# Second MoE's output products in a fused delta-rule, Mish-MoE and hard-swish-MoE kernel: weights stationary, 512 tokens moving

## Chip, cores and metric

One Trainium2 chip, one of its cores. The metric is the device time of the kernel in microseconds. All tensors are float32.

## What is computed

A delta-rule attention over 4 batches, 8 heads, 768 steps and head size 48 gives 3072 tokens of 384 features. Two feed-forward layers follow, each 384 -> 2048 -> 384:

```
h = k_n·state; state += beta * k_n ⊗ (v - h); y_t = q_t · state      (per batch and head, in order of t)
x  = y as (batch * seq, heads * head_dim)                            (3072, 384)
h1 = x @ w1_in;   x2  = (h1 * tanh(softplus(h1))) @ w1_out           first MoE (Mish)
h2 = x2 @ w2_in;  out = (h2 * clip(h2 + 3, 0, 6) / 6) @ w2_out       second MoE (hard-swish)
```

## The kernel before, in words

**Split numbers.** TensorE works on a float32 form of reduced precision (fp32r). Each operand is therefore kept as a high part and a low part, and each product of two float32 matrices is three products: high x high, high x low, low x high. In names, `xh`/`xl` are the parts of the tokens, `wih`/`wil` of the input weights, `ghi`/`glo` of the activated hidden values, `woh`/`wol` of the output weights.

**Blocks and units.** The 3072 tokens go through each MoE in 6 blocks of 512 (`n` is 0 to 5 in the first MoE, 6 to 11 in the second). The 2048 hidden features are 16 slices of 128 (`f`). One block and one slice make a unit, `u = 16 n + f`. A unit has two groups of products:

- hidden products, `mm1` (line 1285): weights are loaded into TensorE (stationary), the 512 tokens move through. 3 slices of the 384 input features x 3 splits = 9 products of 128x512, into one PSUM bank `hps`;
- output products. In the first MoE, `mm2_t` (line 1306): weights stationary, 512 hidden values move, 3 slices of 128 output features x 3 splits = 9 products of 128x512 into three banks `o0` to `o2`, which hold output features in partitions and tokens in columns. In the second MoE, `mm2_second` (line 1444): here the hidden values are stationary, 128 tokens at a time, and the 384 columns of the output weights move: 4 groups of tokens x 3 splits = 12 products of 128x384 into four banks `o0` to `o3` (in the trace `p`), which hold tokens in partitions.

The banks collect over the 16 units of a block. Between hidden and output products ACT and VectorE work on each unit. In the second MoE (`finish2`): ACT `r` (line 1417) and VectorE `r` (line 1419) read `hps` and form the hard-swish, ACT writes `ghi` (line 1291), VectorE writes `glo` (line 1425).

**Ends of blocks.** `flush1` (first MoE) copies the three banks to SBUF and stores them to a DRAM buffer `x2d`, features in partitions; `load_x2` (line 1410) loads a block of it for the second MoE as `x2in`, and `make_x` (lines 1263, 1267) splits it. `flush2` (second MoE, the first five blocks) copies the four banks, two with ACT (line 1459) and two with VectorE (line 1457), into `osb`, and stores them to `out` with four DMAs (line 1464), one for each batch. `last_out` does the same for the last block, cut in two halves. `osb` has three buffers in turn.

**Order.** Every engine executes its instructions in a fixed order. A small planner (`Flow`) writes it: each flow is a Python generator that yields an event to wait for or a tuple of engine and estimated duration, and the planner picks the flow that can begin earliest, corrected by hand-set penalties. `moe` issues the products of the units: the hidden group of unit `u`, then the output group of an earlier one. At a boundary the groups go: two output groups of the old block, the new block's first hidden group, the old block's last output group, two hidden groups in a row, the new block's first output group; elsewhere hidden and output groups alternate. `mm2_t` issues the low products of a unit last, except in the last unit of a block, where it goes bank by bank.

Of the kernel before, what the change touches and what calls it, by code (L numbers as in the profile page):

```python
# [8 lines left out]
F32 = mybir.dt.float32  # L9
# [3 lines left out]
ACTF = mybir.ActivationFunctionType  # L13
# [3 lines left out]
C = 32  # L17
# [126 lines left out]
def tile_delta_rule__moe_mish__moe_hardswish(  # L144
# [12 lines left out]
    nc = tc.nc  # L157
    B, H, S, D = q.shape
    NT, DM = out.shape
    DFF = w1_in.shape[1]  # L160
    KD = DM // 128
    KF = DFF // 128
# [5 lines left out]
    NB = NS // 4  # L168
# [14 lines left out]
    with tc.manual_schedule():  # L183
# [3 lines left out]
        ps_o = ctx.enter_context(tc.tile_pool(name="ps_o", bufs=1, space=bass.MemoryType.PSUM))  # L187
# [963 lines left out]
        wi, wo = {}, {}  # L1151
# [102 lines left out]
        xhl, acc = {}, {}  # L1254
# [36 lines left out]
            nc.scalar.activation(out=hi, in_=g, func=ACTF.Copy)  # L1291
            return hi, lo

        def mm2_t(i, f, hi, lo):
            g, e = divmod(f, 4)
            wh, wl = wo[1, g]
            ops = [(dc, x) for dc in range(KD) for x in range(3)]
            if f < KF - 1:
                ops.sort(key=lambda z: z[1] == 2)
            for n, (dc, x) in enumerate(ops):  # L1300
                if n % 3 == 0:
                    yield "PE", 3 * MM, 0
                if n == 0 and f == 0:
                    acc[i] = [ps_o.tile([128, 512], F32, tag=f"o{z}", name=f"o{z}") for z in range(KD)]
                w, a = ((wh, hi), (wl, hi), (wh, lo))[x]
                nc.tensor.matmul(out=acc[i][dc], lhsT=w[:, e, 128 * dc:128 * (dc + 1)], rhs=a,  # L1306
                                 start=(f == 0 and x == 0), stop=(f == KF - 1 and x == 2))
# [33 lines left out]
        def mm2_first(u):  # L1341
            i, f = divmod(u, KF)
            yield f"lo1.{7 * (f // 4) + KD + f % 4}"
            yield f"g{u}"
            if f == 0 and i:
                yield f"flush{i - 1}"
            if u == 0:
                for b in ("o0", "o1", "o2"):
                    yield lambda: bank_at[b]
            yield from mm2_t(i, f, *gs.pop(u))  # L1350
            flow.set(f"mm2.{u}")
            if f == KF - 1:
                flow.add(flush1(i), pen=-0.2)
# [8 lines left out]
        def moe():  # L1362
# [32 lines left out]
            while done < 2 * NB * KF - 1:  # L1395
                done += 1
                yield from mm2_second(done)
# [31 lines left out]
        def mm2_second(u):  # L1429
            n, f = divmod(u, KF)  # L1430
            g, e = divmod(f, 4)
            yield f"lo2.{7 * g + KD + e}"
            yield f"g{u}"
            if f == 0:
                yield f"flush{n - 1}"
            yield "PE", 12 * 0.1745, 0
            if f == 0:
                acc[n] = [(ps_o if s < 3 else ps_b).tile([128, DM], F32, tag=f"o{s}", name=f"p{s}") for s in range(4)]
            hi, lo = gs.pop(u)
            wh, wl = wo[2, g]  # L1440
            for s in range(4):
                c = slice(128 * s, 128 * (s + 1))
                for x, (a, w) in enumerate(((hi, wh), (hi, wl), (lo, wh))):
                    nc.tensor.matmul(out=acc[n][s], lhsT=a[:, c], rhs=w[:, e, :],  # L1444
                                     start=(f == 0 and x == 0), stop=(f == KF - 1 and x == 2))
            flow.set(f"mm2.{u}")
            if f == KF - 1:
                flow.add((flush2 if n < 2 * NB - 1 else last_out)(n), pen=-0.2)

        def flush2(n):  # L1450
            a, i = acc.pop(n), n - NB
            yield "lo2.27"
            o = p2.tile([128, 4, DM], F32, tag=f"r{i % 3}", name="osb")
            for s in range(4):
                yield ("DVE.", 0.55) if s % 2 else ("ACT", 0.5)
                if s % 2:
                    nc.vector.tensor_copy(out=o[:, s, :], in_=a[s])
                else:
                    nc.scalar.activation(out=o[:, s, :], in_=a[s], func=ACTF.Copy)
            flow.set(f"flush{n}")  # L1460
            yield "SP", 0.3
            for b in range(B):
                r0 = b * S + 128 * i
                nc.sync.dma_start(
                    out=out[r0:r0 + 128, :].rearrange("(t s) d -> s t d", s=C),
                    in_=o[C * b:C * (b + 1)],
                )

        def last_out(n):
            a, i = acc.pop(n), n - NB  # L1470
# [50 lines left out]
        p2 = ps_b = None  # L1521
# [21 lines left out]
        for m, lower, val in ((maskl, True, -1.0), (masku, False, 1.0)):  # L1543
# [4 lines left out]
            for b in range(B):  # L1548
                p = slice(C * b, C * (b + 1))
                nc.gpsimd.tensor_copy(out=m[p, :], in_=lt[p, p])  # L1550
        for b in range(B):
            p = slice(C * b, C * (b + 1))
# [143 lines left out]
```

## Time and profile before

| | |
|---|---|
| median of 3 runs | 1020.66 us (1019.56 to 1022.0) |
| the profiled execution's own time | 1023.31 us |
| its span, from the first to the last instruction | 1021.3 us |
| mean granted TensorE clock | 0.994 of full speed |
| TensorE products, busy | 990.8 us (97%) |
| VectorE / ACT / GpSimd, busy | 646.2 / 487.9 / 87.4 us |
| output products of the second MoE (line 1444) | 1152 of 128x384 |
| second MoE's first output product / last block's first | at 620.40 / 955.00 us |

The profile is of one execution. Products overlap in TensorE's pipeline, so that an instruction's own duration (some 0.34 or 0.39 us) is longer than the distance between two starts; what a product costs is read from starts. In the chain of waits, a piece's start lies at the end of the first product's issue and its length reaches to the next piece, so these pieces can be compared with each other. DVE is VectorE, SPq is the SyncE queue that issues DMAs, PEclk the granted TensorE clock (1.00 is 2.4 GHz).

### The profile page before, as it was taken

The page shows a single profiled execution, that of the slowest core. Times are in us where ns is not written, and L with a number is a line of the kernel's source. Part 1 is how long each engine was busy: PE and PEld are TensorE (multiplying, and loading weights), DVE is VectorE, ACT ScalarE, POOL GpSimd, SP SyncE. Part 2 cuts the span into 40 slices and gives each one's busy share as a digit, 9 for nine tenths or more (in the row PEclk, how much of TensorE's full clock was granted, in tenths as well). Part 3 has the DMA queues.
Part 4 walks back from the last instruction along what each step waited for, and adds up shares of the span by engine and source line. Part 5 has one row for each costly group of instructions (what it writes and reads, how often), then busy time and mean ns, then how long its engine had stood idle before and what let it go on. Part 6 is the DMA issues. An engine that isn't in the chain of part 4 may idle for free.

```text
span 1021.3 us, 29630 instructions
## 1 busy us (share of the span) xinstructions
PE 990.8 (97%) x12563; PEld 828.2 (81%) x12584; DVE 646.2 (63%) x1581; ACT 487.9 (48%) x1164; POOL 87.4 (9%) x132
## 2 busy tenths in 40 slices
PE   7888999999999999999999999999999999999997
PEld 5466777877887887788788888999999989999997
DVE  7999899875887688597527889543343333433432
ACT  4456588736655564564225566343343333433332
POOL 3242112102202110110000000000000000000000
PEclk9998999999999999999999999999999999999999
DMA  4644545245435654543133534011020020200101
GB/s 84 164 90 127 148 117 122 55 80 87 69 83 82 103 117 70 96 91 82 30 103 95 180 125 165 1 31 32 1 62 1 1 62 1 62 1 1 31 1 31
DMA packets 207156, 73.66 MB, mean 72 GB/s; under 512 B 189968, under 2 KB 193040, under 8 KB 207024
## 3 DMA queue, kind: packets, MB, share of 16 engines
q1 hardware_dynamic: 205696, 71.27, 30.7%
q8 instruction: 99, 1.62, 0.7%
q10 hardware_dynamic: 1328, 0.49, 0.2%
q14 instruction: 33, 0.27, 0.1%
HBM read 55.74 MB, written 15.99 MB: 70 GB/s over the span
## 4 chain that ended last, share of the span: by engine, by line
PE 82%; DVE 11%; ACT 3%; issue 2%; DMA 1%; POOL 0%; SPq 0%; DVEq 0%; ACTq 0%; POOLq 0%
PE hps L1285 36%; PE p L1444 20%; PE o L1306 16%; DVE sbd L943 2%; PE ksps L880 1%; PE gps L489 1%; PE dsps L932 1%; PE ups L890 1%; DVE tmp L847 1%; DVE late L708 1%; DVE tw L701 1%; PE yps L880 1%; PE yps L900 1%; DVE tp L851 1%; PE qps L777 1%
## 5 line engine op out<-in xcount | busy, mean ns | idle before, releaser
L1285 PE MATMUL hps<-xh,wih 128*128 128x512 f32 x576 | 229.7, 399 | 3.6 <-ACT mt L511 2.1
L1285 PE MATMUL hps<-xh,wil 128*128 128x512 f32 x576 | 227.0, 394 | 0.0
L1285 PE MATMUL hps<-xl,wih 128*128 128x512 f32 x576 | 226.6, 393 | 0.0
L1419 DVE SCALAR_TENSOR_TENSOR r<-r,hps 128x512 f32<-128x512 f32 x96 | 66.0, 688 | 173.6 <-ACT r L1417 173.5
L1417 ACT ACTIVATE r<-hps,half_c 128x512 f32<-128x512 f32 x96 | 66.1, 689 | 166.2 <-PE hps L1285 166.0
L1285 PEld LDWEIGHTS hps<-xh,wih 128*128 128x128 f32 x576 | 108.4, 188 | 27.2 <-ACT mt L511 2.7
L1444 PE MATMUL p<-woh,glo 128*128 128x384 f32 x384 | 129.5, 337 | 0.0
L1444 PE MATMUL p<-woh,ghi 128*128 128x384 f32 x384 | 129.2, 337 | 0.0
L1444 PE MATMUL p<-wol,ghi 128*128 128x384 f32 x384 | 128.9, 336 | 0.0
L1285 PEld LDWEIGHTS hps<-xh,wil 128*128 128x128 f32 x576 | 108.3, 188 | 23.7 <-DVE wil L1250 0.4
L1285 PEld LDWEIGHTS hps<-xl,wih 128*128 128x128 f32 x576 | 108.4, 188 | 19.3 <-DVE xl L1267 0.3
L1316 ACT ACTIVATE g<-hps 128x512 f32<-128x512 f32 x96 | 57.0, 594 | 127.2 <-PE hps L1285 126.8
L1306 PE MATMUL o<-ghi,wol 128*128 128x512 f32 x288 | 114.3, 397 | 0.0
L1306 PE MATMUL o<-ghi,woh 128*128 128x512 f32 x288 | 114.0, 396 | 0.0
L1325 DVE TENSOR_TENSOR glo<-g,ghi 128x512 fp32r<-128x512 f32 x96 | 66.5, 692 | 59.7 <-ACT ghi L1291 59.0
L1425 DVE TENSOR_TENSOR glo<-r,ghi 128x512 fp32r<-128x512 f32 x96 | 66.5, 693 | 58.9 <-ACT ghi L1291 58.1
L1291 ACT ACTIVATE ghi<-r 128x512 fp32r<-128x512 f32 x96 | 60.7, 632 | 70.1 <-DVE r L1419 70.0
L1306 PE MATMUL o<-glo,woh 128*128 128x512 f32 x288 | 84.1, 393 | 0.0
L1444 PEld LDWEIGHTS p<-woh,ghi 128*128 128x128 f32 x384 | 72.2, 188 | 4.0
L1444 PEld LDWEIGHTS p<-wol,ghi 128*128 128x128 f32 x384 | 72.1, 188 | 3.9
L1444 PEld LDWEIGHTS p<-woh,glo 128*128 128x128 f32 x384 | 72.0, 188 | 0.0
L847 DVE TENSOR_TENSOR tmp<-tp,ash 128x126 f32<-128x126 f32 (+22 forms) x248 | 64.6, 260 | 9.5 <-POOL tp L832 3.3
(151 smaller groups left out, 1358.4 us busy)
## 6 DMA issues: line engine op xcount, KB each, us to landing
raw<-in_moe_w_in_dram SPq DMA_DIRECT2D x24, 512.0 KB, 4.2
raw<-in_moe_w_out_dram SPq DMA_DIRECT2D x32, 384.0 KB, 3.2
vt<-in_v_dram SPq DMA_DIRECT2D x96, 48.0 KB, 2.7
x2d<-x2out SPq DMA_DIRECT2D x6, 768.0 KB, 4.4
x2in<-x2d SPq DMA_DIRECT2D x6, 768.0 KB, 6.1
kpad<-in_k_dram SPq DMA_DIRECT2D x92, 48.0 KB, 2.2
ash<-ad SPq DMA_DIRECT2D x16, 256.0 KB, 3.6
out_dram<-osb SPq DMA_DIRECT2D x20, 192.0 KB, 3.3
```

Source lines behind the costliest of these rows:

```text
L847: nc.vector.tensor_tensor(out=tv, in0=x[:, 0:m, j:j + 1].to_broadcast([128, m, n]), in1=a[:, j:j + 1, j + 1:C].to_broadcast([128, m, n]), ...
L880: nc.tensor.matmul(out=ps[C * b:C * (b + 1), j, :], lhsT=kqt[t][:, b, j, i, :], rhs=sbd[:, b, j, :], start=(i == 0 or j == 0), stop=(i == ...
L943: nc.vector.tensor_tensor(out=o, in0=o, in1=S_part(b, r), op=ALU.add)
L1285: nc.tensor.matmul(out=ps[0], lhsT=w[:, kk, c], rhs=xhl[n][xi][:, kk, :], start=(kk == 0 and x == 0), stop=(kk == KD - 1 and x == 2))
L1291: nc.scalar.activation(out=hi, in_=g, func=ACTF.Copy)
L1306: nc.tensor.matmul(out=acc[i][dc], lhsT=w[:, e, 128 * dc:128 * (dc + 1)], rhs=a, start=(f == 0 and x == 0), stop=(f == KF - 1 and x == 2))
L1316: nc.scalar.activation(out=g, in_=ps, func=ACTF.Mish)
L1325: nc.vector.tensor_tensor(out=lo, in0=g, in1=hi.bitcast(F32), op=ALU.subtract)
L1417: nc.scalar.activation(out=r, in_=ps, func=ACTF.Relu, scale=1.0 / 6.0, bias=half_c)
L1419: nc.vector.scalar_tensor_tensor(out=r, in0=r, scalar=1.0, in1=ps, op0=ALU.min, op1=ALU.mult)
L1425: nc.vector.tensor_tensor(out=lo, in0=r, in1=hi.bitcast(F32), op=ALU.subtract)
L1444: nc.tensor.matmul(out=acc[n][s], lhsT=a[:, c], rhs=w[:, e, :], start=(f == 0 and x == 0), stop=(f == KF - 1 and x == 2))
```

## The change

For the first five blocks of the second MoE (`n < 2*NB - 1`) the output products are issued by the first MoE's `mm2_t`, with the second MoE's weights: weights stationary, 512 hidden values moving, three banks. The sums then have output features in partitions, 128 at a time, and tokens in columns. `flush2` turns them with three VectorE transposes, which turn each 32x32 block of a bank in place; the 128-byte rows that this leaves are put in their places by the store, now 16 DMAs for a block (4 batches x 4 groups of 32 features). The last block is computed and stored as before.

```diff
-        def mm2_t(i, f, hi, lo):
+        def mm2_t(i, f, hi, lo, ph=1):
             g, e = divmod(f, 4)
-            wh, wl = wo[1, g]
+            wh, wl = wo[ph, g]
...
             hi, lo = gs.pop(u)
-            wh, wl = wo[2, g]
-            for s in range(4):
-                c = slice(128 * s, 128 * (s + 1))
-                for x, (a, w) in enumerate(((hi, wh), (hi, wl), (lo, wh))):
-                    nc.tensor.matmul(out=acc[n][s], lhsT=a[:, c], rhs=w[:, e, :],
-                                     start=(f == 0 and x == 0), stop=(f == KF - 1 and x == 2))
+            if n < 2 * NB - 1:
+                yield from mm2_t(n, f, hi, lo, 2)
+            else:
...
         def flush2(n):
             a, i = acc.pop(n), n - NB
             yield "lo2.27"
-            o = p2.tile([128, 4, DM], F32, tag=f"r{i % 3}", name="osb")
-            for s in range(4):
-                yield ("DVE.", 0.55) if s % 2 else ("ACT", 0.5)
-                if s % 2:
-                    nc.vector.tensor_copy(out=o[:, s, :], in_=a[s])
-                else:
-                    nc.scalar.activation(out=o[:, s, :], in_=a[s], func=ACTF.Copy)
+            o = p2.tile([128, KD, 512], F32, tag=f"r{i % 3}", name="osb")
+            for dc in range(KD):
+                yield "DVE.", 0.72
+                nc.vector.transpose(out=o[:, dc, :], in_=a[dc])
             flow.set(f"flush{n}")
-            yield "SP", 0.3
             for b in range(B):
                 r0 = b * S + 128 * i
-                nc.sync.dma_start(
-                    out=out[r0:r0 + 128, :].rearrange("(t s) d -> s t d", s=C),
-                    in_=o[C * b:C * (b + 1)],
-                )
+                for p in range(4):
+                    yield "SP", 0.45
+                    nc.sync.dma_start(
+                        out=out[r0:r0 + 128, :].rearrange("(t s) (d p f) -> s d t p f", s=C, p=4, f=C)[:, :, :, p, :],
+                        in_=o[C * p:C * (p + 1)].rearrange("s d (t b f) -> s d t b f", b=B, f=C)[:, :, :, b, :],
+                    )
```

How the order moves, first on TensorE at the second MoE's first output group (`hps` is the hidden bank, `p` and `o` the output banks, the number tells banks apart). Before, the first two of four token groups:

```order
L1285 MATMUL hps<-xh,wil 128x512
L1444 MATMUL p_10700<-woh,ghi 128x384
L1444 MATMUL p_10700<-wol,ghi 128x384
L1444 MATMUL p_10700<-woh,glo 128x384
L1444 MATMUL p_10701<-woh,ghi 128x384
L1444 MATMUL p_10701<-wol,ghi 128x384
L1444 MATMUL p_10701<-woh,glo 128x384
```

and in the changed kernel, the whole group:

```order
L1285 MATMUL hps<-xh,wil 128x512
L1306 MATMUL o_10700<-ghi,woh 128x512
L1306 MATMUL o_10700<-ghi,wol 128x512
L1306 MATMUL o_10701<-ghi,woh 128x512
L1306 MATMUL o_10701<-ghi,wol 128x512
L1306 MATMUL o_10702<-ghi,woh 128x512
L1306 MATMUL o_10702<-ghi,wol 128x512
L1306 MATMUL o_10700<-glo,woh 128x512
L1306 MATMUL o_10701<-glo,woh 128x512
L1306 MATMUL o_10702<-glo,woh 128x512
L1285 MATMUL hps<-xh,wih 128x512
```

Twelve products of 384 columns have become nine of 512, the three that need `glo` now last. Second, on VectorE at the first of the five boundaries (`glo` and `r` belong to the first unit of the next block). Before:

```order
L1419 SCALAR_TENSOR_TENSOR r_11194<-r_11194,hps 128x512
L1425 TENSOR_TENSOR glo<-r_11194,ghi 128x512
L1457 COPY osb<-p_10701 128x384
L1457 COPY osb<-p_10703 128x384
L1419 SCALAR_TENSOR_TENSOR r_11228<-r_11228,hps 128x512
```

and in the changed kernel:

```order
L1419 SCALAR_TENSOR_TENSOR r_11148<-r_11148,hps 128x512
L1460 STREAM_TRANSPOSE osb<-o_10700 128x512
L1460 STREAM_TRANSPOSE osb<-o_10701 128x512
L1460 STREAM_TRANSPOSE osb<-o_10702 128x512
L1425 TENSOR_TENSOR glo<-r_11148,ghi 128x512
L1419 SCALAR_TENSOR_TENSOR r_11178<-r_11178,hps 128x512
```

The three transposes stand ahead of `glo`, where the two copies stood behind it; ACT's two copies are gone.

## Rows read from the trace of the kernel before

**Rows 1.** The page: busy us and shares; shares of the chain by line.

```profile
PE 990.8 (97%) x12563; PEld 828.2 (81%) x12584; DVE 646.2 (63%) x1581; ACT 487.9 (48%) x1164; POOL 87.4 (9%) x132
...
PE hps L1285 36%; PE p L1444 20%; PE o L1306 16%; DVE sbd L943 2%; PE ksps L880 1%; PE gps L489 1%; PE dsps L932 1%; PE ups L890 1%; DVE tmp L847 1%; DVE late L708 1%; DVE tw L701 1%; PE yps L880 1%; PE yps L900 1%; DVE tp L851 1%; PE qps L777 1%
```

**Rows 2.** Windows by block: length, PE, PEld, DVE, ACT, POOL busy, PEclk, DMA share, GB/s.

```profile
555.12:620.40 65.28, 65.28 (x290) 54.05 (x289) 56.87 (x116) 40.32 (x75) 0.00 (x0) 1.00 0.48 156
620.40:687.33 66.93, 66.93 (x338) 60.69 (x337) 39.95 (x71) 30.08 (x51) 0.00 (x0) 1.00 0.16 52
687.33:754.25 66.92, 66.92 (x337) 60.67 (x337) 24.81 (x37) 23.43 (x38) 0.00 (x0) 1.00 0.09 24
754.25:821.16 66.91, 66.91 (x337) 60.67 (x337) 24.80 (x37) 23.42 (x38) 0.00 (x0) 1.00 0.09 24
821.16:888.09 66.93, 66.93 (x338) 60.69 (x337) 24.81 (x37) 23.44 (x38) 0.00 (x0) 1.00 0.09 24
888.09:955.00 66.91, 66.91 (x337) 60.67 (x337) 24.80 (x37) 23.42 (x38) 0.00 (x0) 1.00 0.09 24
955.00:1021.30 66.30, 60.70 (x310) 55.27 (x308) 21.07 (x31) 19.59 (x31) 0.00 (x0) 0.98 0.07 20
```

**Rows 3.** Chain of waits, end of the first MoE: start us, us, what.

```profile
567.37 2.04 PE o L1306 x9
569.40 2.04 PE hps L1285 x9
...
616.33 4.08 PE hps L1285 x18
620.40 2.10 PE p L1444 x12
```

**Rows 4.** Chain of waits, second MoE.

```profile
754.25 2.10 PE p L1444 x12
756.35 2.08 PE hps L1285 x9
```

**Rows 5.** Timeline, PE at a boundary: start us, us, engine, line, instruction.

```profile
749.96 0.39 PE L1285 MATMUL hps<-xh,wih 128*128 128x512 f32 x1
...
752.04 0.39 PE L1285 MATMUL hps<-xh,wih 128*128 128x512 f32 x1
...
754.08 0.33 PE L1444 MATMUL p<-woh,ghi 128*128 128x384 f32 x1
```

**Rows 6.** Timeline, DVE at the same boundary.

```profile
748.84 0.69 DVE L1419 SCALAR_TENSOR_TENSOR r<-r,hps 128x512 f32<-128x512 f32 x1 [2.52 <-ACT r L1417]
750.23 0.69 DVE L1425 TENSOR_TENSOR glo<-r,ghi 128x512 fp32r<-128x512 f32 x1 [0.70 <-ACT ghi L1291]
750.84 1.01 DVE L1457 COPY osb<-p 128x384 f32<-128x384 f32 x2
753.02 0.69 DVE L1419 SCALAR_TENSOR_TENSOR r<-r,hps 128x512 f32<-128x512 f32 x1 [1.17 <-ACT r L1417]
```

**Rows 7.** Groups of instructions, DVE: the transposes; busy us, mean ns.

```profile
L355 DVE STREAM_TRANSPOSE kqt<-qpad 128x512 f32<-128x512 f32 x24 | 16.8, 702 | 1.0 <-DMA qpad<-in_q_dram 0.9
L1083 DVE STREAM_TRANSPOSE y<-yps 128x384 f32<-128x384 f32 x12 | 7.0, 581 | 7.9 <-PE yps L900 7.9
L761 DVE STREAM_TRANSPOSE late<-late 128x1024 f32<-128x1024 f32 x1 | 2.0, 2017 | 0.0
```

**Rows 8.** Timeline, SP queue at the first boundary.

```profile
685.00 2.27 SPq L1464 DMA_DIRECT2D out_dram<-osb  x4
687.32 0.85 SPq L1410 DMA_DIRECT2D x2in<-x2d  x1
```

**Rows 9.** Tile y, the issues of its stores: ns min/median/max.

```profile
L1094 SPq DMA_DIRECT2D xt<-y x48: 302/476/1652, 306.3 to 526.9; - x48
```

**Rows 10.** DMA issues: count, KB each, median us to landing.

```profile
xt<-y SPq DMA_DIRECT2D x48, 48.0 KB, 1.9
```

**Rows 11.** Timeline, ACT: first reader of the x2in load of rows 8.

```profile
741.79 0.63 ACT L1263 ACTIVATE xh<-x2in 128x512 fp32r<-128x512 f32 x1 [2.05 <-PE hps L1285]
```

More of the change, by code (lines that the diff above doesn't have):

```diff
@@ L1435, in mm2_second @@
                 yield f"flush{n - 1}"
-            yield "PE", 12 * 0.1745, 0
-            if f == 0:
-                acc[n] = [(ps_o if s < 3 else ps_b).tile([128, DM], F32, tag=f"o{s}", name=f"p{s}") for s in range(4)]
             hi, lo = gs.pop(u)
-            wh, wl = wo[2, g]
-            for s in range(4):
-                c = slice(128 * s, 128 * (s + 1))
-                for x, (a, w) in enumerate(((hi, wh), (hi, wl), (lo, wh))):
-                    nc.tensor.matmul(out=acc[n][s], lhsT=a[:, c], rhs=w[:, e, :],
-                                     start=(f == 0 and x == 0), stop=(f == KF - 1 and x == 2))
+            if n < 2 * NB - 1:
+                yield from mm2_t(n, f, hi, lo, 2)
+            else:
+                yield "PE", 12 * 0.1745, 0
+                if f == 0:
+                    acc[n] = [(ps_o if s < 3 else ps_b).tile([128, DM], F32, tag=f"o{s}", name=f"p{s}")
+                              for s in range(4)]
+                wh, wl = wo[2, g]
+                for s in range(4):
+                    c = slice(128 * s, 128 * (s + 1))
+                    for x, (a, w) in enumerate(((hi, wh), (hi, wl), (lo, wh))):
+                        nc.tensor.matmul(out=acc[n][s], lhsT=a[:, c], rhs=w[:, e, :],
+                                         start=(f == 0 and x == 0), stop=(f == KF - 1 and x == 2))
             flow.set(f"mm2.{u}")
```

## The prediction

> **What bounds the kernel now.** I read the busy shares first, then the chain of waits, then a table of windows cut at the block boundaries, then single instructions around one boundary. The page says that TensorE's products are busy for 97% of the span, and the chain that ended last runs through TensorE for most of it, 20% through the line that is changed [rows 1]. The chain in the second MoE is nothing but products, so what counts is how long a group of products takes from its start to the start of the next group. The windows say that TensorE is busy for the whole of each block, at a granted clock of 1.00 (2.4 GHz) [rows 2].
>
> The reader should compare two stretches. In the last block of the first MoE no attention work is left, and each unit is nine products of 512 columns for the hidden layer and nine of 512 for the output: 2.04 us and 2.04 us [rows 3]. In the second MoE a unit is the same nine hidden products and twelve output products of 384 columns: 2.08 and 2.10 us [rows 4]. Both units move 9 x 512 + 4608 columns, since 12 x 384 = 9 x 512 = 4608. Yet the block of 16 units takes 65.28 us in the one and 66.91 to 66.93 us in the other [rows 2].
>
> Why the hidden products, which the diff leaves alone, also take 2.08 instead of 2.04 can be narrowed down. At a boundary two hidden groups stand in a row: the nine right behind a 384-column group go from 749.96 to 752.04 us, 2.08 us, and the nine behind those from 752.04 to 754.08, 2.04 us [rows 5]. Same second-MoE weights, same tokens, same clock; only what went ahead differs. And the pair at the start of the second MoE, which follows 512-column products, takes 4.08 us for 18, clean throughout [rows 3]. So the excess of 0.04 us hangs on the 384-column group ahead.
>
> **The change, part by part.** *Products.* 80 units (5 blocks of 16) lose twelve products of 384 columns and get nine of 512, in the order of the first MoE's output products. The price I take is that of the stretch that already looks so: a block of 65.28 us. The five blocks take 66.93 + 66.92 + 66.91 + 66.93 + 66.91 = 334.60 us now and 5 x 65.28 = 326.40 us then: **8.2 us less**. Split by groups it is 80 x (2.10 - 2.04) = 4.8 us for the output products themselves and 75 x (2.08 - 2.04) = 3.0 us for the hidden groups that stand behind one (15 in each block; the sixteenth is the second of a pair, which is clean already); the missing 0.4 is rounding of the rows. The block of comparison carries more other load than those that change (VectorE 56.87 us busy against 24.8, DMA share 0.48 against 0.09) [rows 2], so nothing there was easier. The last block, 955.00 to the end, keeps its products.
>
> *A rule against it.* The rows give 175 ns for a 384-column product (2.10 / 12) and 227 ns for a 512-column one in the clean stretch (2.04 / 9). The Trainium skill, "TensorE: Matmul & The Clock Gate", section "Back-to-back issue gap", puts the warm gap at N / 2.4 + 2.5 ns, which is 162.5 and 215.8 ns; by it twelve and nine products differ by 8 ns a unit, an estimate of 0.6 us over 80 units and no gain that can be measured. The trace disagrees with both figures, by 12 ns and 11 ns.
>
> *Sums out of PSUM.* Per block two ACT copies and two VectorE copies go, and three VectorE transposes of 128x512 come, in one row on one engine. The trace has no such transpose from PSUM at this size. From below: 0.70 us, the 128x512 one out of SBUF; in between: 0.581 us for 128x384 out of PSUM, which by columns makes 0.775; from above: the slowest one, 2.017 us for 1024 columns, makes 1.01 [rows 7]. I take 0.78, by the row that also reads PSUM. Three make 2.3 us. The order puts them ahead of the unit's glo instruction, which used to come first. Is there room? VectorE finishes the instruction ahead at 748.84 + 0.69 = 749.53 us [rows 6]; the first two banks are complete before the third, since a block's last unit goes bank by bank; the third is complete when the group ends at 749.96. So the transposes end near 751.9 and glo near 752.6, instead of 750.92. The next user of the banks is the group that starts at 754.08 [rows 5], glo itself is only wanted by that group's seventh product, 1.36 us later, and the next VectorE instruction, at 753.02 [rows 6], is not pushed. Cost: **nothing**, covered by the pair of hidden groups. If a transpose took the 1.01 us of the upper bound, glo would end at 753.25 and the next instruction would slip by 0.2 us, with over 3 us until its result is used.
>
> *Stores.* Each block's store becomes 16 issues of 48 KB in 128-byte pieces instead of four of 192 KB in 1536-byte pieces. The kernel already has such issues, the 48 stores to xt: 0.476 us each on the SP queue [rows 9], 1.9 us to landing [rows 10]. Sixteen are 7.6 us against 2.27 [rows 8], and the transposes end about 1.5 us later than the copies did, so the x2in load queued behind moves from 687.32 to about 694. It is first read at 741.79 [rows 11], and at the slowest issue of rows 9 (1.652 x 16 = 26 us) it would still be issued by 714. Landing one after another the stores would take 30 us of a 66 us block, and the last such block is through more than 30 us before the end of the span. Cost: nothing; its cover is the more than 40 us between that load and its first reader, and were that gone, each block would start late by what is missing.
>
> *Order.* No row of any engine moves ahead of the second MoE. Inside it one weight conversion changes place with its neighbour on VectorE, and one on ACT, in a block in which TensorE never waits [rows 2].
>
> **Sum.** The profiled execution took 1023.31 us, 2.65 above the median of the runs shown; less 8.2 it is 1015.1. On the median: 1020.66 - 8.2 = **1012.5 us**. A measurement of this kernel can tell about 0.2%, 2 us, from no change.
>
> **Rivals.** *Only the columns count, chance 0.08.* If a 512-column product in the second MoE simply costs what the hidden ones cost there now, 2.08 us for nine, the new group saves 2.10 - 2.08 = 0.02 us, 1.6 us in all: 1019.1, no change that can be measured. The rule of the Trainium skill cited above would put it near there too; rows 3 and 4 speak against both its figures. For it: every single hidden group of the steady stretch reads 2.08 [rows 4]. Against: the clean second nines of rows 5 and the clean 18 of rows 3 use the second MoE's weights.
>
> *Only the output products gain, chance 0.09.* If the hidden groups stay at 2.08 because of the alternation of lines or operands and not of 384 columns, 4.8 us is left: 1015.9. Against: the first MoE alternates in the same way at 2.04 [rows 3].
>
> *The turns hold the banks, chance 0.04: slower.* All three sums now pass through VectorE ahead of glo. TensorE would first wait for glo: it is due at 754.08 + 1.36 = 755.44, and it ends at 749.53 + 3t + 0.69, so waiting begins at a transpose of t = 1.74 us. At t = 2.5 each boundary costs 3 x 0.76 = 2.3 us, 11.4 over five, and the time is 1020.66 - 8.2 + 11.4 = 1023.9. For it: nothing here shows a 512-column transpose from PSUM. Against: it needs over twice the upper bound.
>
> **Numbers.** The forecast has 0.79. The range, 1011.2 to 1016.0, takes in the spread of the runs below (1.1 us) and the case of the output products alone above, and leaves out the two others. Faster 0.88 (forecast and second rival), same 0.08, slower 0.04.
>
> **What would show it.** Right: blocks of about 65.3 us for the five, output groups and hidden groups both at 2.04 us in the chain, a last block of 66.3 us as before, transposes of 0.7 to 0.8 us, no idle time on TensorE at the boundaries. Wrong: hidden groups still at 2.08 (second rival), new groups at 2.08 (first rival), or products that wait for a transpose or for glo at five places (third).

## The result and the profile after

| | before | changed kernel |
|---|---|---|
| median, 6 runs each | 1020.88 us (1019.35 to 1022.0) | 1012.2 us (1010.14 to 1016.56) |
| ratio, 95% interval | | 0.992 (0.9897 to 0.9943) |
| the profiled execution, time and span | 1023.31, 1021.3 us | 1010.14, 1008.4 us |

The kernel became faster by 8.7 us, and the 1012.5 us that were forecast lie 0.3 us from the median (6.4 us lie between its quickest and its slowest run). The windows of the changed kernel, cut in the same way as [rows 2] (columns as there; the first is again the last block of the first MoE, the last the unchanged last block):

```profile
550.54:615.82 65.28, 65.28 (x289) 54.07 (x289) 56.83 (x116) 40.45 (x75) 0.00 (x0) 1.00 0.48 157
615.82:681.10 65.28, 65.28 (x289) 54.07 (x289) 40.51 (x72) 29.30 (x49) 0.00 (x0) 1.00 0.15 49
681.10:746.38 65.28, 65.28 (x289) 54.07 (x289) 25.56 (x38) 22.67 (x36) 0.00 (x0) 1.00 0.12 25
...
876.94:942.22 65.28, 65.28 (x289) 54.07 (x289) 25.56 (x38) 22.67 (x36) 0.00 (x0) 1.00 0.12 25
942.22:1008.40 66.18, 60.69 (x309) 55.26 (x308) 21.08 (x31) 19.59 (x31) 0.00 (x0) 1.00 0.11 23
```

The five blocks take 942.22 - 615.82 = 326.40 us where they took 334.60: 8.20 us less, each block as long as the first MoE's. The two profiled spans differ by 12.9 us, and the rest of that is not the change: 4.6 us lie ahead of the second MoE's first output product, at 615.82 instead of 620.40 us, where no instruction has changed. In the kernels of this study, all the same up to there, that product starts between 614.35 and 624.65 us. Whoever compares one profiled execution with one other must cut the windows at the change.

The chain of waits of the changed kernel, against [rows 3, 4]:

```profile
742.30 4.08 PE hps L1285 x18
746.38 2.04 PE o L1306 x9
748.42 2.04 PE hps L1285 x9
...
942.22 2.10 PE p L1448 x12
944.32 2.08 PE hps L1285 x9
```

Output groups and hidden groups both take 2.04 us, and at 942.22, with the first 384-column group of the last block, both old numbers are back at once.

VectorE at a boundary, against [rows 6] (start us, us, engine, line, instruction):

```profile
741.08 0.69 DVE L1419 SCALAR_TENSOR_TENSOR r<-r,hps 128x512 f32<-128x512 f32 x1 [2.38 <-ACT r L1417]
741.68 1.91 DVE L1460 STREAM_TRANSPOSE osb<-o 128x512 f32<-128x512 f32 x3
743.51 0.65 DVE L1425 TENSOR_TENSOR glo<-r,ghi 128x512 fp32r<-128x512 f32 x1
745.16 0.69 DVE L1419 SCALAR_TENSOR_TENSOR r<-r,hps 128x512 f32<-128x512 f32 x1 [1.00 <-ACT r L1417]
```

The transposes are over at 743.59 and glo at 744.16, and the block's next output group starts at 746.38 in the chain; VectorE still waits 1.00 us before its next instruction. Of the tile `osb` (ns min/median/max) and of the SP queue at the first boundary, against [rows 7 to 9]:

```profile
L1466 SPq DMA_DIRECT2D out_dram<-osb x80: 594/618/1542, 678.3 to 949.8; - x80
L1460 DVE STREAM_TRANSPOSE osb<-o x15: 672/674/710, 676.4 to 938.8; 128x512 f32<-128x512 f32 x15
```

```profile
678.33 11.58 SPq L1466 DMA_DIRECT2D out_dram<-osb  x16
690.02 0.59 SPq L1410 DMA_DIRECT2D x2in<-x2d  x1
```

Sixteen issues hold the queue for 11.58 us. The x2in load behind them goes out at 690.02 and is first read at 734.17 us, 44 us later; such a load takes 5.0 us to land (median of six).

### The profile page after: what moved, and what is told of

It reads as the page before. It is cut to its first block, busy times and chain, and to the rows that moved or that the text cites. A ratio compares the mean times of both kernels' runs of the same rounds, so it can differ in the third digit from the quotient of the medians.

```text
span 1008.4 us, 29226 instructions
## 1 busy us (share of the span) xinstructions
PE 981.7 (97%) x12344; PEld 792.1 (79%) x12344; DVE 649.5 (64%) x1586; ACT 483.9 (48%) x1154; POOL 88.2 (9%) x132
## 4 chain that ended last, share of the span: by engine, by line
PE 73%; DVE 6%; issue 1%; DMA 1%; ACT 1%; SPq 0%; POOL 0%; DVEq 0%; ACTq 0%; POOLq 0%
PE hps L1285 34%; PE o L1306 30%; PE p L1448 3%; DVE tmp L847 2%; DVE tp L851 2%; DVE sbd L943 1%; PE ksps L880 1%; PE ups L890 1%; PE gps L489 1%; PE yps L900 1%; PE dsps L932 1%; PE yps L880 1%; DVE glo L1325 1%; DMA td<-tp 1%; DVE kqt L355 0%
## 5 line engine op out<-in xcount | busy, mean ns | idle before, releaser
L1306 PE MATMUL o<-ghi,wol 128*128 128x512 f32 x528 | 207.0, 392 | 0.0
L1306 PE MATMUL o<-ghi,woh 128*128 128x512 f32 x528 | 206.6, 391 | 0.0
L1306 PE MATMUL o<-glo,woh 128*128 128x512 f32 x528 | 153.1, 391 | 0.0
L1306 PEld LDWEIGHTS o<-ghi,wol 128*128 128x128 f32 x528 | 99.1, 188 | 20.7
L1306 PEld LDWEIGHTS o<-ghi,woh 128*128 128x128 f32 x528 | 99.1, 188 | 20.5
L1306 PEld LDWEIGHTS o<-glo,woh 128*128 128x128 f32 x528 | 98.4, 188 | 20.9
L851 DVE TENSOR_TENSOR tp<-tp,tmp 128x126 f32<-128x126 f32 (+22 forms) x248 | 64.9, 262 | 7.1
L1291 ACT ACTIVATE ghi<-g 128x512 fp32r<-128x512 f32 x96 | 60.4, 629 | 2.2
L943 DVE TENSOR_TENSOR sbd<-sbd,dsps 48x192 f32<-48x192 f32 x152 | 53.3, 351 | 6.0 <-PE dsps L932 3.3
```

Source lines behind the costliest of these rows:

```text
L851: nc.vector.tensor_tensor(out=x[:, 0:m, j + 1:C], in0=x[:, 0:m, j + 1:C], in1=tv, op=ALU.subtract)
L943: nc.vector.tensor_tensor(out=o, in0=o, in1=S_part(b, r), op=ALU.add)
```

## The experiments

**Which operand, or which width?** The change swaps two things at once: the weights become the stationary operand, and 512 columns move instead of 384. Theory A says that the width is all; theory B that the stationary operand, or the order that comes with it, matters. Two kernels change one of them alone.

Tokens stationary as before, 512 columns moving:

```diff
+            wide = NB < n < 2 * NB - 1
...
+            d0 = min(DM * e, 4 * DM - 512)
-            for s in range(4):
+            for s in range(len(acc[n])):
...
-                    nc.tensor.matmul(out=acc[n][s], lhsT=a[:, c], rhs=w[:, e, :],
+                    nc.tensor.matmul(out=acc[n][s], lhsT=a[:, c],
+                                     rhs=w.rearrange("p e d -> p (e d)")[:, d0:d0 + 512] if wide else w[:, e, :],
...
```

> The kernel before (tokens stationary), but in blocks 7 to 10 of the second MoE's 6 to 11 the moving operand is 512 columns wide instead of 384 and the fourth group of 128 tokens is left out: nine products of 128x512 instead of twelve of 128x384, so a part of the output is not computed and its columns take in weights of a neighbouring slice. Theory A (what counts is the width of the moving operand, not which operand is stationary): output groups and hidden groups both take 2.04 us, the four blocks about 65.3 us each, block 6 stays at 66.9. Theory B (weights-stationary order, or which tensor is loaded, makes the difference): the groups stay at 2.08 to 2.10 us and the blocks at 66.9.

Windows and chain, first the block that stayed and one that changed:

```profile
619.81:686.73 66.92, 66.92 (x337) 60.68 (x337) 39.93 (x71) 30.08 (x51) 0.00 (x0) 1.00 0.17 52
686.73:752.01 65.28, 65.28 (x289) 54.05 (x289) 24.79 (x37) 23.43 (x38) 0.00 (x0) 1.00 0.09 25
```

```profile
682.61 4.12 PE hps L1285 x18
686.73 2.04 PE p L1447 x9
688.77 2.04 PE hps L1285 x9
```

Theory A to the hundredth: 65.28 us for each of the four blocks with tokens stationary, and the hidden groups at 2.04 too.

Weights stationary as in the change, 384 columns moving:

```diff
-            ops = [(dc, x) for dc in range(KD) for x in range(3)]
+            m, per = (512, 3) if ph == 1 else (384, 4)
+            ops = [(dc, x) for dc in range(KD) for x in range(per)]
...
-                nc.tensor.matmul(out=acc[i][dc], lhsT=w[:, e, 128 * dc:128 * (dc + 1)], rhs=a,
+                nc.tensor.matmul(out=acc[i][dc][:, 0:m], lhsT=w[:, e, 128 * dc:128 * (dc + 1)], rhs=a[:, 0:m],
...
```

> The changed kernel (weights stationary), but in the five blocks only the first 384 of the 512 tokens move and the products with the low part of the hidden values are issued twice: twelve products of 128x384 in place of nine of 128x512, the same 4608 columns; so the sums are wrong in part and the last 128 tokens of a block are not computed. Theory A (width of the moving operand): the blocks go back to about 66.9 us, output groups to 2.10 and the hidden groups behind them to 2.08 us. Theory B (weights-stationary order): the blocks stay at about 65.3 us, hidden groups at 2.04.

Chain and window:

```profile
888.22 2.10 PE o L1307 x12
890.33 2.08 PE hps L1285 x9
```

```profile
888.22:955.14 66.92, 66.92 (x338) 60.68 (x337) 25.76 (x41) 22.67 (x36) 0.00 (x0) 1.00 0.11 24
```

The whole gain is gone, hidden groups included. With both kernels theory B has fallen: swapping the operands neither helps nor is needed, it is only the way to get 512 columns into one product when the output has 384 features. Both kernels collect into three banks, so the number of banks does not matter either. With 4608 columns in a group, however, the width also sets the number of products; the two are told apart further down.

**What does a narrower product cost?** The kernel of the last experiment with 256 columns and six products in place of three (`m, per = (512, 3) if ph == 1 else (256, 6)`).

> The changed kernel, but only 256 tokens move and there are eighteen products of 128x256 a unit in the five blocks, again 4608 columns; half the tokens are not computed. Theory A1 (each product costs its columns at 2.4 GHz and a fixed 13 to 15 ns, worked out from 227 ns at 512 and 175 ns at 384): 256 columns cost 120 to 122 ns, a group of eighteen 2.16 to 2.20 us, a block 67.2 to 68.5 us with the effect on the hidden group behind. Theory A2 (the weight load, 188 ns busy in the groups of instructions, is a floor under narrow products): a group takes up to 18 x 0.188 = 3.4 us and a block some 87 us.

```profile
894.65 2.15 PE o L1307 x18
896.80 2.07 PE hps L1285 x9
```

```profile
894.65:962.15 67.50, 67.50 (x433) 61.54 (x433) 25.73 (x41) 22.64 (x36) 0.00 (x0) 1.00 0.11 24
```

A1 holds but for 0.01 us in the group (2.15 against 2.16 to 2.20), A2 falls: 2.15 / 18 = 119 ns a product, far below the 188 ns for which a weight load shows as busy in the groups of instructions. Loads of that shown length evidently overlap, so they are no floor at 256 columns.

A group in alternation always follows products of another width. At the end of a block two output groups stand in a row, and the second can be read by itself; first the kernel with 256 columns, then the one with 384:

```profile
882.01 4.31 PE o L1307 x36
```

```profile
875.73 4.18 PE o L1307 x24
```

The second eighteen take 4.31 - 2.15 = 2.16 us, 120.0 ns each, and the second twelve 4.18 - 2.10 = 2.08 us, 173.3 ns each; at 512 columns it is 2.04 / 9 = 226.7 ns throughout. From 256 to 512 that is 0.417 ns a column, which is 1 / 2.4 GHz, and a product has 13.3 ns on top at each of the three widths. So twelve products of 384 take 0.04 us more than nine of 512 because they are three more. The rest of their 0.06 us, some 0.02, is lost only where they follow 512-column products, and the 0.04 us of the hidden group only where it follows a 384-column one. Of the 8.2 us, 80 x 0.04 = 3.2 come from having fewer products and the other 5.0 from widths that no longer alternate.

**Are the transposes hidden, and how much room is left?** The transposes of the change, done twice and four times over:

```diff
-            for dc in range(KD):
+            for dc in list(range(KD)) * 2:
```

> The changed kernel with every one of the three transposes of a block done twice (six at a boundary; the output is unchanged). In the changed kernel's trace the transposes start at 741.68 us of a boundary, three take 1.91 us, glo follows, and glo is wanted at about 747.6 us. Theory A (the transposes are hidden and have room): six end near 745.5, glo near 746.2, TensorE never waits, the blocks stay at 65.28 us. Rival (the boundary has little room and the transposes hold TensorE up): blocks of over 65.8 us with TensorE idle before the first output products of a block.

VectorE at a boundary, and a window:

```profile
743.62 0.69 DVE L1419 SCALAR_TENSOR_TENSOR r<-r,hps 128x512 f32<-128x512 f32 x1 [2.38 <-ACT r L1417]
744.23 3.69 DVE L1460 STREAM_TRANSPOSE osb<-o 128x512 f32<-128x512 f32 x6
747.85 0.65 DVE L1425 TENSOR_TENSOR glo<-r,ghi 128x512 fp32r<-128x512 f32 x1
```

```profile
683.64:748.92 65.28, 65.28 (x290) 54.05 (x289) 27.20 (x42) 22.59 (x35) 0.00 (x0) 1.00 0.12 25
```

Twice the transposes cost nothing: that they are hidden is shown, with room for at least three more than the change needs. Four times over (`* 4`):

> The changed kernel with the three transposes of a block done four times over (twelve at a boundary; the output is unchanged). Theory A (the room at a boundary is what the prediction worked out from the low products of the next block's first unit): twelve end near 749.3 us on the scale of the changed kernel's boundary, glo ends near 750.0 where it is wanted at 747.6, so TensorE idles about 2.4 us at each of five boundaries, 12 us in all, and the blocks take about 67.7 us. Rival (banks and VectorE have more room than that): blocks of 65.3 us.

The wait of TensorE, the chain at a boundary and a window:

```profile
PE o L1306 <- DVE osb L1460: 6.2, 4, 1.5
```

```profile
744.72 6.02 DVE osb L1460 x10
750.73 0.14 issue
750.87 2.62 PE o L1306 x9
```

```profile
683.43:750.87 67.44, 65.90 (x289) 53.74 (x289) 30.82 (x48) 22.59 (x35) 0.00 (x0) 1.00 0.12 24
```

The size is nearly right, 67.44 - 65.28 = 2.2 us a boundary against 2.4, but not the place. TensorE first waits 1.5 us for the tenth transpose, the last one that reads the first bank. The rest is lost among the group's nine products, and little of it to glo, as the starts of products and weight loads (PEld) at this boundary show:

```profile
750.87 0.47 PE L1306 MATMUL o<-ghi,woh 128*128 128x512 f32 x1 [1.54 <-DVE osb L1460]
752.54 0.95 PE L1306 MATMUL o<-glo,woh 128*128 128x512 f32 x3
753.33 0.39 PE L1285 MATMUL hps<-xh,wih 128*128 128x512 f32 x1
```

```profile
751.37 0.19 PEld L1306 LDWEIGHTS o<-ghi,woh 128*128 128x128 f32 x1 [0.24 <-DVE osb L1460]
751.97 0.19 PEld L1306 LDWEIGHTS o<-ghi,woh 128*128 128x128 f32 x1 [0.30 <-DVE osb L1460]
752.54 0.52 PEld L1306 LDWEIGHTS o<-glo,woh 128*128 128x128 f32 x3 [0.28 <-DVE glo L1425]
```

The nine take 2.46 us from the first start to the next group's instead of 2.04 (the chain's 2.62 reaches 0.16 us further). The six ahead of the first low product take 1.67 us instead of 1.36, as the loads for the second and the third bank wait for transposes too; the three low ones lose 0.11. With transposes repeated over all banks the banks are what comes free late; the expectation had only counted up to glo. Over all five boundaries it is more than the 12 us expected: the last three output groups start at 1011.97 instead of 996.64 us, and less the 0.79 us by which the second MoE began later (616.61 against 615.82) that is 14.5 us. Four boundaries at 2.1 to 2.2 make 8.6, so the fifth cost about 6. The old form of the last block wants glo with its third product instead of its seventh, so TensorE waits 1.54 us for the bank, issues two products and waits 1.10 us again. In the stretch with the second wait the granted clock falls (0.82 in its window), and the windows show what it costs:

```profile
953.13:954.81 1.68, 0.58 (x2) 0.27 (x2) 1.68 (x4) 0.00 (x0) 0.00 (x0) 0.82 0.00 0
954.81:958.38 3.57, 3.57 (x11) 3.57 (x12) 2.53 (x4) 1.84 (x3) 0.00 (x0) 0.50 0.29 47
958.38:961.74 3.36, 3.36 (x10) 2.65 (x10) 0.00 (x0) 0.00 (x0) 0.00 (x0) 0.61 0.50 75
961.74:963.83 2.09, 2.09 (x13) 2.09 (x13) 0.69 (x1) 1.30 (x2) 0.00 (x0) 1.00 0.48 80
```

At 0.50, which is 1.2 GHz, the ten output products left take 3.57 us, and the hidden group behind them 3.36 instead of 2.08 at 0.61. At the other four boundaries, with one wait of 1.5 us and short ones behind it, the clock stays at 1.00.

**Should the last block change too?** All six blocks weights-stationary, the end of the last one as in `flush2`, its stores on two queues:

```diff
-            if n < 2 * NB - 1:
-                yield from mm2_t(n, f, hi, lo, 2)
-            else:
...
+            yield from mm2_t(n, f, hi, lo, 2)
...
+                    (nc.scalar if p % 2 else nc.sync).dma_start(
...
```

> The changed kernel with the last block computed in the same way too: weights stationary, three transposes behind the last product, sixteen stores of 128-byte pieces, eight on the SP queue and eight on ACT's. Theory A: the last block's products gain 16 x 0.1 = 1.6 us, but behind the last product come a transpose (0.9 us with the start), eight issues of 0.62 us on each queue (5.0 us) and a landing of 2.1 us, together about 8 us where the kernel before and the changed one need 5.5; so the end comes about 0.9 us later than with the last block as it was. Rival (issues on two queues run down faster and the products' gain wins): up to 1.6 us earlier.

The last block's window, and its issues and transposes (tile `osb`):

```profile
940.75:1009.60 68.85, 59.16 (x262) 48.64 (x260) 22.06 (x32) 18.60 (x29) 0.00 (x0) 0.97 0.15 21
```

```profile
L1469 SPq DMA_DIRECT2D out_dram<-osb x8: 590/623/717, 1000.7 to 1005.4; - x8
L1469 ACTq DMA_DIRECT2D out_dram<-osb x8: 598/637/791, 1000.7 to 1005.9; - x8
L1464 DVE STREAM_TRANSPOSE osb<-o x3: 716/717/717, 998.6 to 999.9; 128x512 f32<-128x512 f32 x3
```

The products gain what they should (TensorE is busy 59.16 instead of 60.69 us), yet the block takes 68.85 us instead of 66.18, 2.7 us longer; 0.9 had been expected. From the first transpose at 998.6 to the end at 1009.6 are 11.0 us, where the block as it was needs 5.5 behind its last product. The expectation had all three parts but let a single transpose stand behind the last product: all three do here (998.6 to 1000.7), the eight issues take 5.8 us, to 1006.5, not 5.0, and the span ends 3.1 us behind that, not 2.1. So the last block is better left as it was.

**Fewer changes of width in the last block.** The excess sits on the first hidden group behind a 384-column group, so pairing the groups should cut it:

```diff
-                while done < u - (1 if f in (0, KF - 1) else 2):
+                while (n < 2 * NB - 1 or f % 2 or not f) and done < u - (1 if f in (0, KF - 1) else 2):
```

> The changed kernel with the last block's groups in pairs: two hidden groups, two output groups of 384 columns, and so on, in place of strict alternation; the output is unchanged. In the kernel before two output groups in a row take 4.18 us and two hidden groups behind them 4.12, against 2 x 2.10 and 2 x 2.08 in alternation. Theory A (the excess of 0.04 us sits only on the first hidden group behind a 384-column group, and a second output group in a row is cheaper by 0.03): with some seven fewer changes from 384 to 512 columns the stretch from the last output group of the block ahead to the end, 72.30 us in the changed kernel (936.10 to 1008.40), takes about 71.8. Rival (the excess goes with every hidden group between 384-column groups): 72.3.

```profile
941.11 6.12 PE hps L1285 x27
947.23 4.18 PE p L1448 x24
951.42 4.12 PE hps L1285 x18
```

The stretch ends at 1011.0 and starts at 941.11 - 2.04 = 939.07 us: 71.9 us instead of 72.3, where theory A has about 71.8. The products are the same, only their groups change places, so this bears out that a change of width has a price of its own. It is the quickest end of all that were tried, but 0.4 us can be told from nothing only in the trace; a single run, at 1012.84 us, cannot show it.

**The change once more.** Unaltered, six more runs.

> The changed kernel unaltered, timed once more against the kernel before on one chip. If the gain is the five blocks' 8.2 us and nothing else, the ratio is 0.992 within some 0.002, with the five blocks at 65.28 us each in the profile.

1011.16 us against 1020.45, a ratio of 0.9909 (0.9888 to 0.9931). The forecast ratio of 0.992 lies in both intervals, and the five blocks take 326.40 us in this profile too (616.77 to 943.17).

## Why the prediction was right

**Products, 8.2 us.** Measured 8.20 us in the windows. It came from reading the price off a stretch of the same kernel that already did what the change would do, and not off an instruction's duration. The split also holds: new groups at 2.04 us, and hidden groups, which the diff does not touch, back from 2.08 to 2.04. That the excess hangs on the 384-column group ahead had been argued from two rows of a boundary; the kernels with one property changed show it. What the prediction lacked is that part of the 384-column group's own price is of the same kind: it took the whole of 2.10 / 12 = 175 ns for the price of a product, where 173.3 is the product and the rest the change of width. The sum is right all the same, because the stretch it was read off does not alternate. That the median lies only 0.3 us from the forecast is in part luck: six more runs of the same kernel had theirs at 1011.16.

**The rule against it.** The Trainium skill, "TensorE: Matmul & The Clock Gate", section "Back-to-back issue gap", gives N / 2.4 + 2.5 ns, which leaves 8 ns a unit. The section calls that the gap of an isolated product, and for a stream of products with their weight loads it states about 131 ns at 512 columns; the trace agrees with neither. In a row of one width it shows 226.7, 173.3 and 120.0 ns where the rule has 215.8, 162.5 and 109.2. Above what the columns alone take at 2.4 GHz that is 13.3 ns for a product, not 2.5, so the number of products counts more than the rule lets it, and the rule has no term for a change of width.

**Rivals.** "Only the columns count" (1019.1) and "only the output products gain" (1015.9) fell with the chain above. "The turns hold the banks" was to begin at 1.74 us a transpose, 5.2 us for three, which is 1.7 times the upper bound of 1.01. The changed kernel's three take 1.91 us; six take 3.69 and cost nothing, twelve cost 14.5 us.

**Transposes, taken at 0.78 us.** They take 0.67, below even the lower bound of 0.70 that was read off a transpose out of SBUF. The row nearest in kind (PSUM, 128x384, 0.581 us) misled because it was scaled by columns: a third more columns cost 0.09 us, not the 0.19 of the scaling. It cost nothing, as the cover is larger than either.

**Stores, sixteen issues of 0.476 us.** They take 0.618 at the median and 11.58 us in a row instead of 7.6. The pieces are 128 bytes long in both, so the length alone does not set the price of an issue; which property does was not tried. The prediction also had the transposes end 1.5 us later than the copies; but in [rows 6] the copies end at 751.85, where it put the transposes' end at 751.9. In the event the stores start 0.4 us earlier, 2.8 us ahead of the next block's first output group (678.33 and 681.10) instead of 2.3 (685.00 and 687.33). The load behind them went out about 2 us later in the block than forecast, and with its 5 us to land it still had some 39 us to spare.

**Last block, unchanged.** 66.18 us after 66.30.

## What to carry to other kernels

Read the price of a product from the distance of starts in a stretch that looks like the change, and look at the neighbours too: a group of 384-column products cost 0.06 us more than its columns in 512-column products, and the group behind it paid another 0.04. If an output width does not fill the moving operand, swap the operands so that the long dimension moves, and pay for the turned result with an engine that has time. Where two widths must stay, put groups of the same width in a row. At the end of the kernel nothing hides the turn and its small stores; keep the direct form there.

## What the runs showed that was not expected

A change of width has a price of its own. In a row of one width each product takes its columns and 13.3 ns, whether 256, 384 or 512 columns. But twelve products of 384 behind products of 512 take some 0.02 us more than in a row, and the nine 512-column products behind them 0.04 us more; eighteen of 256 are no dearer behind products of 512 (2.15 against 2.16 us) and slow the nine behind them by 0.03 (2.07 us). The slowing is over within one group: the second group of a pair is clean in each of these kernels. What lies behind it was not settled; the experiments only show that it goes with a change in the width of the moving operand and not with which tensor is stationary. Nor do they tell whether the 13.3 ns belong to the product or to its weight load, as every product here has a load of its own (289 of each in a block).

And one boundary cost more than its waits: at the fifth boundary of the kernel with four times the transposes two waits, 2.6 us together, were followed by a stretch at half the granted clock, and about 6 us were lost in all.
